# Two decode layers on one core: evacuation order, the place of the residual row, and what fills the waits between the layers

## The chip, the core and the metric

The kernel runs on one core of a Trainium2 chip, in one launch. The metric is the device time of that launch in microseconds. Everything is float32. Five engines work beside each other, each through its own instructions in program order: TensorE (PE) multiplies, VectorE (DVE) and ScalarE (ACT) do elementwise work, GpSimd (POOL) sets constants, and SyncE (SP) issues nearly all DMAs. They wait for each other by semaphores.

## The reference

Eight sequences (B = 8), one new token each, width D = 1024, go through the same pair of sublayers twice. Attention has 32 query heads over 4 key/value heads of size 128 and a cache of 4096 positions; the feed-forward width is 3584.

```
def _A_ref(x, k_cache, v_cache, wq, wo):
    q = (x @ wq) split into 32 heads of 128
    scores = q . k * Dh**-0.5;  p = softmax(scores);  o = p . v
    return o @ wo
def _B_ref(x, w1, b1, w2, b2):
    return gelu(x @ w1 + b1) @ w2 + b2
x = x + _A_ref(layernorm(x)); x = x + _B_ref(layernorm(x))
x = x + _A_ref(layernorm(x)); x = x + _B_ref(layernorm(x))
```

Both layers use the same weights and the same caches. The caches hold 8 x 4 x 4096 x 128 numbers each, 64 MiB per cache, and they are read in both layers, except for six value pieces of the last sequence that stay in SBUF.

## The kernel before, in words

**Memory.** One SBUF tile, the arena, is cut into 52 units of 1024 columns (4 KB in each of 128 partitions, 0.5 MiB in all). All weights and cache blocks come into it. A list, `stream`, names the transfers in the order in which they are issued, with the units where each may land; `pump` (L226) issues the head of the list once its units are free, and `release` (L238) frees the units of a block that has been read. All of it is decided while the program is built: on the chip, SP goes through a fixed order, and an issue waits for the last PE instruction that read the units. A transfer that waits therefore holds up all those behind it in the list.

**Rows.** Because there are only 8 sequences, a row vector of 1024 is held as `x_row`, 128 partitions by 256: the four column quarters lie under each other, 32 partitions each, of which 8 are used. Products are spread the same way: four matmuls that write to partitions 0, 32, 64 and 96 of one PSUM bank use the four column quarters of TensorE. The layer's input is also kept turned, in `xnT` (by `layernorm`, L192), 8 tiles of 128 x 8, which is what the matmuls take as their left side. PSUM is shared out as one bank each under the names "s" and "pt" and two under "o", and a bank is written again only after it has been read.

**Attention** (L578) goes sequence by sequence over k blocks (`scores`), a softmax (`probs`, `turn`) and v blocks (`values`, `heads`). `hooks` are functions put behind a named step. `project` (L334) multiplies with wo and adds to `x_row`.

**Feed-forward.** `expand` (L252) makes the 3584 hidden values in 7 groups of 512. For a group, eight matmul rounds over w1 write to `acc`; `flush` (L168) runs what is in `pending`; then DVE and ACT each copy one half of `acc` out of PSUM, scaled (L269, L270), into one of two row buffers, and the group's `hidden_group` (L319) is put in `pending`. `hidden_group` turns the row by four transposes on PE (L278) and does the bias and GELU in seven small steps on DVE and ACT (L324 to L330), which leaves `hT`. So a group's GELU is done behind the matmuls of the next group and ahead of its evacuation.

**The turn between the layers** is `swap` (L388). It works through four column blocks c of w2. Each block has 28 k tiles in three transfers: "u" (tiles 0 to 3), 0 (tiles 4 to 19) and 1 (tiles 20 to 27), in an order set by `W2_ORDER`. For a block, `down` (L367) does 28 matmuls (L371), DVE copies the result (L404), PE sums the partition groups (L406), and DVE adds it to the turned row (L408). One more matmul (L409) carries the block's result to the residual row, added to `x_row` at L430. The block gives two of the 8 k tiles of the next layer's query product, which is done at once by `q_part` (L287, L293) for two halves u: four pieces of wq in each block. wq has been in the arena since the start, and its units are what the next w2 blocks and then the next layer's k blocks are loaded into. The list behind the w1 groups is: w2 of blocks 0 to 3, k of the last sequence in several pieces, among them a rest of 64 KB of wq ("qe", unit 0, ahead of the third k piece), and so on. The k tile 7 of wq had to leave the arena: one half was parked in PSUM at the start (`park`, L616) and comes back by `unpark` (L623), an ACT copy and then a DVE copy, behind piece (3, 1), into the units that this piece frees; most of the other half is in `spare`, and the rest is "qe". `moments` (L450) forms the layer norm's statistics behind the last block, and the query rows are turned into `qz`.

**The bias b2.** `bias_row` (L351) builds the row b2 with products on PE and adds it to `x_row` in layer 0, behind the first group of `expand`; in layer 1 it writes to `b2_row`.

**Layer 1's feed-forward** has its w2 in the arena but for four "u" blocks of 0.5 MiB, which are the last transfers. `work` (L744) puts `grow(u - 1)`, the w2 products of a finished group, and `flush` behind a group's evacuation. Behind the last group come `grow_u(0, 1)`, the products of "u" for column quarters 0 and 1, then `flush` (the last group's turns and GELU), then `grow_u(2, 3)`; the last group's own products, the add (L748) and the store follow.

Of the kernel before, what the change touches and what calls it, by code (L numbers as in the profile page):

```python
# [8 lines left out]
F32 = mybir.dt.float32  # L9
# [5 lines left out]
P = 128  # L15
# [89 lines left out]
def decode_layers(ctx: ExitStack, tc: tile.TileContext, x, kc, vc, wq, wo, w1, w2, out):  # L105
# [12 lines left out]
    bits = const.tile([P, 2 + B + 2 * HQ + REP + T + 18], F32, name="bits")  # L118
# [8 lines left out]
    ones = ones.to_broadcast([P, P])  # L127
    epst = bit(1)
# [19 lines left out]
    xv = xv[:, :, 0:B]  # L148
    nc.gpsimd.memset(qz, 0.0)
# [42 lines left out]
    def layernorm(xr, rsum):  # L192
# [5 lines left out]
        shift = oxT[:, HQ * B + NT * XS + PAD:]  # L198
# [53 lines left out]
    def expand(name, rs, work={}):  # L252
        rows = [row_s, qz[:, 2 * GT * B:2 * GT * B + CH]]
        for u in range(NGR):
            acc = ps_o.tile([P, CH], F32, tag="o", name="acc")
            kt = 0
            for i, slot in enumerate(tiles((name, u))):
# [6 lines left out]
                flush()  # L264
# [3 lines left out]
            row = rows[u % 2]  # L268
            nc.vector.tensor_scalar(row[:, 0:CH // 2], acc[:, 0:CH // 2], rs, None, op0=ALU.mult)  # L269
            nc.scalar.activation(row[:, CH // 2:], acc[:, CH // 2:], AF.Copy, scale=rs)  # L270
            pending.append(lambda u=u, row=row: hidden_group(u, row))
# [79 lines left out]
    def bias_row(out, add, dg):  # L351
# [8 lines left out]
        if add is None:  # L360
            nc.vector.tensor_copy(out, y[:, 0:Q4])
        else:
            nc.vector.tensor_tensor(out, add, y[:, 0:Q4], ALU.add)
# [3 lines left out]
    def down(y, c, kts):  # L367

        for n, kt in enumerate(kts):
            g = kt % 4  # L370
            nc.tensor.matmul(y[32 * g:32 * g + 32], hT[:, kt * B:kt * B + 32], w2_at[c, kt], start=(n < 4), stop=(n >= NFT - 4))  # L371
# [16 lines left out]
    def swap():  # L388

        flush()  # L390
        ys = small_ps("s")
        nc.vector.tensor_tensor(xv, xv, b2T.unsqueeze(2).to_broadcast([P, NT, B]), ALU.add)
        pt = small_ps("pt")
        acc = q_acc()
        stats = ()
        for c in range(CB):
            y = ys[:, c % 2 * Q4:(c % 2 + 1) * Q4]
            kts = []
            for kind in W2_ORDER[c]:
                kts += arrive(c, kind)  # L400
            down(y, c, kts)
            release(held.pop(("w2u0", c)))
            ysb = row_s[:, c % 2 * Q4:(c % 2 + 1) * Q4]
            nc.vector.tensor_copy(ysb, y)  # L404
            for i in range(2):
# [3 lines left out]
            nc.tensor.matmul(pt[32 * c:32 * c + 32, Q4:2 * Q4], sel_x, ysb, start=True, stop=True)  # L409
            if c == CB - 1:  # L410
                stats = moments(pt)
            for kt in (2 * c, 2 * c + 1):
                for u in range(2):
                    if kt < NT - 1:
                        slot = held.pop(("q", kt, u))
                        q_part(acc, u, kt, 0, slot.ap)
                        release(slot)
                    elif u == 0:
                        q_part(acc, u, kt, 0, spot.ap)
# [399 lines left out]
```

## Time and profile before

| what | value |
|---|---|
| median of 3 runs | 862.34 us (861.06 to 862.88) |
| the profiled execution's own time | 861.24 us |
| its span in the profile | 859.5 us |
| mean granted TensorE clock | 0.803 |
| busy share PE, PEld, DVE, ACT | 63%, 22%, 23%, 7% |
| read from HBM | 358.83 MB, 418 GB/s over the span |

The profile is one execution. Times in it are microseconds from the start of the span. PE is matmuls, PEld is the loading of their left sides; an fp32 matmul shows as two records. In a row of the timeline stand the start, the time, the engine and line, the operation with output and inputs, the shapes and the number of instructions merged; brackets give the idle time before it and what ended it. In the chain of waits each row gives the start and length of what the end of the program hung on. In the table by windows, each engine has its busy time and its number of instructions, and the last three columns are PE's granted clock, the mean busy share of the 16 DMA engines and the rate.

### The profile page before, as it was taken

To read this page: it belongs to the slowest core of one execution; us is meant where nothing else is said; L and a number is where in the kernel's file an instruction comes from. 1 tells how busy PE (TensorE), PEld (TensorE's weight loads), DVE (VectorE), ACT (ScalarE), POOL (GpSimd) and SP (SyncE) were. 2 spreads that over 40 slices of the span, in tenths; PEclk is the share of its full clock that TensorE was granted. 3 is DMA by queue.
4 is the path that set the end of the run, shared out by engine and by line. 5 is a ranking of instruction groups with operands and counts; after the bars stand their busy time and mean duration, and the time that the engine had idled before them with its cause. 6 is when DMAs were issued, how large, how long until landed. Compare 5 with 4: busy or idle time off the path is not lost.

```text
span 859.5 us, 9291 instructions
## 1 busy us (share of the span) xinstructions
PE 540.7 (63%) x3986; PEld 186.6 (22%) x3986; DVE 199.9 (23%) x692; ACT 63.4 (7%) x136; POOL 2.1 (0%) x12
## 2 busy tenths in 40 slices
PE   0766655666655755756688676755656483664687
PEld 0221121121212121322233221111211121121233
DVE  0012231222212122301311332132222132231032
ACT  0110000000000000001101100000000000000020
POOL 0000000000000000000000000000000000000000
PEclk9976787867777777788889886679778687686899
DMA  9999999999999999999999999999999999999994
GB/s 397 432 422 436 432 422 435 425 432 423 432 436 423 432 434 427 425 426 427 416 362 420 378 434 424 445 423 435 428 429 422 432 426 438 430 444 419 422 421 167
DMA packets 19768, 359.55 MB, mean 418 GB/s; under 512 B 2192, under 2 KB 2576, under 8 KB 3600
## 3 DMA queue, kind: packets, MB, share of 16 engines
q1 hardware_dynamic: 19584, 358.82, 98.2%
q8 instruction: 31, 0.51, 0.2%
q10 hardware_dynamic: 144, 0.15, 0.0%
q14 instruction: 9, 0.07, 0.0%
HBM read 358.83 MB, written 0.13 MB: 418 GB/s over the span
## 4 chain that ended last, share of the span: by engine, by line
DMA 73%; PE 23%; DVE 1%; issue 1%; another core or an unknown queue 1%; ACT 0%; SPq 0%; ACTq 0%; DVEq 0%
DMA arena<-in_v_dram 27%; DMA arena<-in_k_dram 23%; DMA arena<-in_wo_dram 10%; PE o_ps L544 8%; DMA arena<-in_w_dram 7%; PE sps L488 7%; DMA arena<-in_wq_dram 6%; PE y L340 1%; PE sps L377 1%; PE acc L260 1%; PE acc L293 1%; PE sps L520 1%; PE sps L371 1%; PE sps L278 1%
## 5 line engine op out<-in xcount | busy, mean ns | idle before, releaser
L544 PE MATMUL o_ps<-arena 128*32 128x512 f32 x1024 | 169.4, 791 | 80.6 <-DMA arena<-in_v_dram 80.6
L488 PE MATMUL sps<-arena,qz 128*32 128x512 f32 x1024 | 149.6, 727 | 97.1 <-DMA arena<-in_k_dram 94.4
L488 PEld LDWEIGHTS sps<-arena,qz 128*32 128x32 f32 x1024 | 33.0, 126 | 180.0 <-DMA arena<-in_k_dram 101.4
L549 DVE SCALAR_TENSOR_TENSOR scr<-o_ps,bits,scr 128x128 f32<-128x128 f32 x192 | 67.4, 351 | 6.8
L544 PEld LDWEIGHTS o_ps<-arena 128*32 128x32 f32 x1024 | 34.2, 133 | 147.1 <-issue 113.9
L547 DVE TENSOR_SCALAR scr<-o_ps,bits 128x128 f32<-128x128 f32 x64 | 22.5, 351 | 173.0 <-PE o_ps L544 173.0
L511 ACT ACTIVATE arena<-arena,bits 128x512 f32<-128x512 f32 x32 | 22.8, 714 | 525.9 <-DVE scr L506 525.9
L340 PE MATMUL y<-arena,oxT 128*32 128x256 f32 x512 | 39.9, 469 | 32.8 <-DMA arena<-in_wo_dram 32.8
L493 DVE TENSOR_SCALAR_CACHE_REDUCE arena<-sps 128x512 f32<-128x512 f32 x32 | 22.1, 692 | 150.1 <-PE sps L488 150.1
L520 PE MATMUL sps<-ident,arena 128*128 128x128 f32 x128 | 29.6, 395 | 24.6 <-ACT arena L511 24.3
L260 PE MATMUL acc<-arena,oxT 128*32 128x512 f32 x224 | 34.0, 719 | 11.9 <-DMA arena<-in_w_dram 11.5
L293 PE MATMUL acc<-arena,oxT 128*32 128x512 f32 (+1 forms) x250 | 34.2, 657 | 7.1 <-DMA arena<-in_wq_dram 6.7
L556 PEld LDWEIGHTS sps<-bits,scr 128*128 128x128 f32 x128 | 21.1, 207 | 67.3 <-issue 38.4
L340 PEld LDWEIGHTS y<-arena,oxT 128*32 128x32 f32 x512 | 18.4, 130 | 51.9 <-DMA arena<-in_wo_dram 36.7
L520 PEld LDWEIGHTS sps<-ident,arena 128*128 128x128 f32 x128 | 21.3, 198 | 29.8 <-ACT arena L511 29.7
L557 DVE TENSOR_TENSOR oxT<-sps,scr 128x8 f32<-128x8 f32 x64 | 10.6, 165 | 72.1 <-PE sps L556 72.1
L556 PE MATMUL sps<-bits,scr 128*128 128x8 f32 x128 | 26.9, 283 | 0.0
L502 PE MATMUL sps<-scr,bits 128*128 128x128 f32 x32 | 8.3, 344 | 22.8 <-DVE scr L498 22.8
L524 DVE COPY arena<-sps 128x512 f32<-128x512 f32 x16 | 11.1, 692 | 30.4 <-PE sps L520 30.4
L377 PE MATMUL sps<-arena,oxT 128*32 128x256 f32 x224 | 16.9, 381 | 0.7 <-DVE oxT L330 0.6
L371 PE MATMUL sps<-arena,oxT 128*32 128x256 f32 x224 | 16.1, 412 | 1.4 <-DMA arena<-in_w_dram 1.4
L195 PE MATMUL sps<-ident,xb 128*128 128x128 f32 x6 | 1.5, 345 | 24.3 <-DMA xb<-in_x_dram 23.2
(116 smaller groups left out, 221.5 us busy)
## 6 DMA issues: line engine op xcount, KB each, us to landing
arena<-in_v_dram SPq DMA_DIRECT2D x19, 4096.0 KB, 19.3
arena<-in_k_dram SPq DMA_DIRECT2D x31, 2048.0 KB, 17.3
arena<-in_k_dram SPq DMA_DIRECT2D x12, 4096.0 KB, 17.5
arena<-in_w_dram SPq DMA_DIRECT2D x17, 2048.0 KB, 12.4
arena<-in_v_dram SPq DMA_DIRECT2D x4, 6144.0 KB, 25.0
arena<-in_v_dram SPq DMA_DIRECT2D x11, 2048.0 KB, 20.0
arena<-in_wo_dram SPq DMA_DIRECT2D x10, 2048.0 KB, 12.6
arena<-in_k_dram SPq DMA_DIRECT2D x2, 6144.0 KB, 23.4
```

What stands on the lines that cost most here:

```text
L260: nc.tensor.matmul(acc[32 * j:32 * j + 32, :], xnT[:, kt * XS:kt * XS + 32], slot.ap[:, c:c + G], start=(kt < 4), stop=(kt >= NT - 4))
L293: nc.tensor.matmul(acc[u][32 * j:32 * j + 32, d0 - j * CH:d1 - j * CH], xnT[:, kt * XS:kt * XS + 32], ap[:, d0 - c0:d1 - c0], start=(kt == ...
L340: nc.tensor.matmul(y[32 * j:32 * j + 32, 0:Q4], lhs[:, n * B:n * B + 32], slot.ap[:, c + j * Q4:c + (j + 1) * Q4], start=(n == 0), stop=(n ...
L371: nc.tensor.matmul(y[32 * g:32 * g + 32], hT[:, kt * B:kt * B + 32], w2_at[c, kt], start=(n < 4), stop=(n >= NFT - 4))
L377: nc.tensor.matmul(y[32 * c:32 * c + 32], hT[:, kt * B:kt * B + 32], w2_at[c, kt], start=st["y0"][c], stop=(kt == NFT - 1))
L488: nc.tensor.matmul(ps[32 * g:32 * g + 32, :], qz[:, c:c + 32], kt[:, g * CH:(g + 1) * CH], start=(j == 0), stop=(j == HKV - 1))
L511: nc.scalar.activation(part, part, AF.Exp, bias=bias, scale=1.0, accum_out=ls[:, h:h + 1])
L520: nc.tensor.transpose(pp[:, t * P:(t + 1) * P], row[:, c:c + P], ident)
L544: nc.tensor.matmul(o[32 * g:32 * g + 32, :], s[:, g], v[:, g * CH:(g + 1) * CH], start=(half == 0), stop=(half == NH - 1))
L547: nc.vector.tensor_scalar(r, o[:, 0:P], sel_t[:, 0:1], None, op0=ALU.mult)
L549: nc.vector.scalar_tensor_tensor(r, o[:, t * P:(t + 1) * P], sel_t[:, t:t + 1], r, op0=ALU.mult, op1=ALU.add)
L556: nc.tensor.matmul(po[:, 0:REP], r_s[j % 2], sel_h, start=True, stop=True)
```

## The change

Line numbers shift by a few; the prediction uses those of before.

1. `expand` takes `lag`. In layer 0 a group is evacuated first and `flush` (its predecessor's turns and GELU) follows. For group 0, the pending variance is flushed ahead of the evacuation, as before in both layers.
2. `swap` begins with the four "u" products of block 0, ahead of the `flush` that turns the last group.
3. Pieces (1, 1) and (3, 1) of wq are kept back (`late`) and done behind the next block's 28 products, between the issue of the DVE copy and the sums that read it. With (3, 1) goes its `unpark`, on ACT and DVE.
4. The product L409, the add L430 and layer 0's `bias_row` are gone. In layer 1 a new `rebuild` makes `x_row` from `xnT` by 16 matmuls of 32 x 128 and a DVE copy, behind the second value piece of the second sequence (number 6). It undoes the mean by a product with the row `shift`, kept now right behind the tiles of `xnT`, and a constant `share` of -1/128.
5. "qe" goes to unit 1 and is put in the list right behind w2, ahead of the k pieces.
6. In layer 1, the last group is turned directly behind its evacuation, and "u" is done for all four column quarters in one go behind it.

The order of the other transfers is as before.

```
-    def expand(name, rs, work={}):
+    def expand(name, rs, lag, work={}):
...
                 release(slot)
-                flush()
                 for f in work.get((u, i), ()):
                     f()
...
             row = rows[u % 2]
+            if u == 0:
+                flush()
             nc.vector.tensor_scalar(row[:, 0:CH // 2], acc[:, 0:CH // 2], rs, None, op0=ALU.mult)
             nc.scalar.activation(row[:, CH // 2:], acc[:, CH // 2:], AF.Copy, scale=rs)
+            if lag:
+                flush()
             pending.append(lambda u=u, row=row: hidden_group(u, row))
...
+    def rebuild():
+
+        ps = small_ps("s")
+        for kt in range(NT):
+            out = ps[32 * (kt // 2):32 * (kt // 2) + 32, kt % 2 * P:(kt % 2 + 1) * P]
+            nc.tensor.matmul(out, xnT[:, kt * XS:kt * XS + 32], ident, start=True, stop=False)
+            nc.tensor.matmul(out, xnT[:, NT * XS:NT * XS + 32], share, start=False, stop=True)
+        nc.vector.tensor_copy(x_row, ps[:, 0:Q4])
...
     def swap():
 
-        flush()
         ys = small_ps("s")
+        down(ys[:, 0:Q4], 0, arrive(0, "u"), 0)
+        flush()
...
+        def used(kt, u):
+            slot = held.pop(("q", kt, u))
+            q_part(acc, u, kt, 0, slot.ap)
+            release(slot)
+            if (kt, u) == (3, 1):
+                st["unparked"] = unpark()
...
             nc.vector.tensor_copy(ysb, y)
+            while late:
+                late.pop()()
             for i in range(2):
                 nc.tensor.matmul(pt[:, i * B:(i + 1) * B], ysb[:, i * P:(i + 1) * P], bsel, start=True, stop=True)
...
-            nc.tensor.matmul(pt[32 * c:32 * c + 32, Q4:2 * Q4], sel_x, ysb, start=True, stop=True)
...
                     if kt < NT - 1:
-                        slot = held.pop(("q", kt, u))
-                        q_part(acc, u, kt, 0, slot.ap)
-                        release(slot)
+                        late.append(lambda kt=kt, u=u: used(kt, u))
+                        if c == CB - 1 or (kt, u) not in ((1, 1), (3, 1)):
+                            late.pop()()
...
-                if kt == 3:
-                    spot = unpark()
-        nc.vector.tensor_tensor(x_row, x_row, pt[:, Q4:2 * Q4], ALU.add)
...
-    qe = (("qe", 0), 1, wq[0][:, -W:-KEEP], (0,), ())
+    qe = (("qe", 0), 1, wq[0][:, -W:-KEEP], (1,), ())
+    stream.append(qe)
     batch(1, last_b, ((4, 16), (4, 20), (4, 24), (2, 0), (2, 16)), ((4, 18),))
-    stream.insert([e[0] for e in stream].index((1, ("k", *k_at(last_b, 4)))), qe)
...
-            ("v", *v_at(last_b - 2, 0)): lambda: bias_row(b2_row, None, spare[:, Q4:Q4 + CH])}
+            ("v", *v_at(last_b - 2, 0)): lambda: bias_row(b2_row, spare[:, Q4:Q4 + CH]),
+            ("v", *v_at(last_b - 1, 1)): rebuild}
...
-            expand("i0", rs, {0: [lambda: bias_row(x_row, x_row, qz[:, 2 * GT * B:2 * GT * B + CH])]})
+            expand("i0", rs, True)
...
-                    (NGR - 1, 0): [lambda: grow(NGR - 2)], NGR - 1: [lambda: grow_u(0, 1), flush, lambda: grow_u(2, 3)]}
-            expand("i1", rs, work)
+                    (NGR - 1, 0): [lambda: grow(NGR - 2)], NGR - 1: [flush, lambda: grow_u(*range(CB))]}
+            expand("i1", rs, False, work)
```

More of the change, by code (lines that the diff above doesn't have):

```diff
@@ L117, in decode_layers @@
     make_identity(nc, ident)
-    bits = const.tile([P, 2 + B + 2 * HQ + REP + T + 18], F32, name="bits")
+    bits = const.tile([P, 3 + B + 2 * HQ + REP + T + 18], F32, name="bits")
     used = [0]
@@ L127, in decode_layers @@
     ones = ones.to_broadcast([P, P])
+    share = bit(1)
+    nc.gpsimd.memset(share, -1.0 / P)
+    share = share.to_broadcast([P, P])
     epst = bit(1)
@@ L359, in bias_row, with down @@
                 nc.tensor.matmul(y[32 * j:32 * j + 32, 0:Q4], ones[:, 0:32], dg[:, j % 2 * Q4:(j % 2 + 1) * Q4], start=True, stop=True)
[L360 to L363, printed above, removed]
+        nc.vector.tensor_copy(out, y[:, 0:Q4])
     w2_at = {}
-    def down(y, c, kts):
-        for n, kt in enumerate(kts):
+    def down(y, c, kts, n0=0):
+        for n, kt in enumerate(kts, n0):
             g = kt % 4
```

12 lines of the change are left out of this document (7 added, 5 removed).

## The prediction

> **What bounds the kernel now.** I read the page first: DMA in 40 slices, its queues, the shares of the chain that ended last.
>
> ```profile
> GB/s 397 432 422 436 432 422 435 425 432 423 432 436 423 432 434 427 425 426 427 416 362 420 378 434 424 445 423 435 428 429 422 432 426 438 430 444 419 422 421 167
> ...
> q1 hardware_dynamic: 19584, 358.82, 98.2%
> ...
> DMA 73%; PE 23%; DVE 1%; issue 1%; another core or an unknown queue 1%; ACT 0%; SPq 0%; ACTq 0%; DVEq 0%
> ```
>
> One queue moves 358.82 MB at a rate that hardly varies, so time is lost only where the rate falls: in slices 21 and 23 (362 and 378), and in the last slice (167), where the transfers end before the program does. Slices 21 and 23 are the turn between the layers (swap). The table by windows cuts it finer; its last columns are PE's granted clock, the DMA share and GB/s.
>
> ```profile
> core 0: us, PE busy (x) PEld busy (x) DVE busy (x) ACT busy (x) POOL busy (x), PEclk, DMA share, GB/s
> 430.62:434.03 3.41, 3.40 (x16) 0.59 (x16) 0.00 (x0) 0.09 (x1) 0.00 (x0) 0.50 1.04 436
> 434.03:437.45 3.42, 1.28 (x11) 0.71 (x8) 1.63 (x7) 0.70 (x2) 0.00 (x0) 1.00 0.96 407
> 437.45:440.86 3.41, 3.41 (x30) 1.54 (x34) 1.38 (x7) 0.23 (x1) 0.58 (x1) 0.50 1.04 442
> 444.50:450.00 5.50, 5.50 (x79) 2.40 (x72) 0.00 (x0) 0.00 (x0) 0.00 (x0) 1.00 0.70 222
> 476.00:478.00 2.00, 1.26 (x10) 0.30 (x2) 1.12 (x6) 0.60 (x2) 0.00 (x0) 1.00 0.92 291
> 482.00:490.00 8.00, 6.21 (x56) 2.07 (x56) 2.59 (x10) 0.00 (x0) 0.00 (x0) 1.00 0.98 334
> 510.00:660.00 150.00, 91.10 (x576) 28.18 (x568) 38.91 (x129) 8.46 (x20) 0.00 (x0) 0.77 1.01 431
> 660.00:810.00 150.00, 87.09 (x692) 30.72 (x688) 30.79 (x105) 6.35 (x15) 0.00 (x0) 0.77 1.00 429
> ```
>
> Against 429 GB/s the three dips lose 5.5 x (1 - 222/429) = 2.65 us, 2 x (1 - 291/429) = 0.64 us and 8 x (1 - 334/429) = 1.77 us: 5.07 us. From 510 to 810 the rate is 431 and 429: a transfer that starts earlier there stays earlier to the end.
>
> Why the first dip: the chain of waits in the turn, as it ended.
>
> ```profile
> 442.66 0.44 DVE scr L404
> ...
> 443.14 0.62 PE sps L406 x4
> ...
> 443.79 0.19 DVE oxT L408
> ...
> 444.02 0.40 PE sps L409
> 444.42 3.71 PE acc L293 x29
> ```
>
> After the first column block (its matmuls end at 442.66) PE waits 1.36 us for the copy, the sums and the add, spends 0.40 us on the residual's product (L409), and only then reads the four wq pieces (3.71 / 4 = 0.93 us each) whose slots the next w2 blocks need. The first of these is issued here, and the answer of the DMA view for that one issue gives its landing:
>
> ```profile
> 445.54 0.33 SPq L233 DMA_DIRECT2D arena<-in_w_dram  x1
> ```
> ```profile
> arena<-in_w_dram SPq DMA_DIRECT2D x1, 512.0 KB, 3.9
> ```
>
> 0.52 MB at 429 GB/s are 1.2 us; the other 2.7 us of the 3.9 are the most that lies between an issue and its data. So an issue must lead the end of the queued data by 2 to 2.7 us.
>
> **The change, part by part.**
>
> *Evacuation ahead of GELU (layer 0).* The turn's start:
>
> ```profile
> 434.15 0.66 PE L278 MATMUL sps<-ident,qz 128*128 128x128 f32 x4
> 436.24 0.48 DVE L269 TENSOR_SCALAR scr<-acc,bits 128x256 f32<-128x256 f32 x1
> 436.83 0.47 ACT L270 ACTIVATE scr<-acc,bits 128x256 f32<-128x256 f32 x1 [0.76 <-DVE scr L269]
> 437.93 4.65 PE L371 MATMUL sps<-arena,oxT 128*32 128x256 f32 x56
> ```
>
> The last group's matmuls end by 434.2; its rows leave PSUM at 436.24, behind the GELU of group 5. Now DVE goes at 434.2, ACT ends about 435.3, and the four turns end at 436.0 instead of 437.93. In between stand the four "u" products of block 0 (4 of 28). What is late next is a transfer:
>
> ```profile
> 427.69 0.33 SPq L233 DMA_DIRECT2D arena<-in_w_dram  x1
> ```
> ```profile
> arena<-in_w_dram SPq DMA_DIRECT2D x1, 2048.0 KB, 9.0
> ```
>
> These 16 w2 tiles land at 427.69 + 9.0 = 436.7, the next eight (1.05 MB, 2.44 us) at 439.2. The 28 products took 4.65 us, of which those up to 440.86 at clock 0.50: 2.93 / 2 + 1.72 = 3.19 us at full clock, 0.114 us each. Sixteen from 436.75 end at 438.6, eight from 439.2 at 440.1. That counts on full clock after 437.45: the rows above show 0.50 behind a window with 1.28 us of 3.42 busy and 1.00 behind one with 3.40; the window 434 to 437.45 will hold some 2.6 us. At half clock the end is 441.4. So block 0 ends 2.5 us (1.2) earlier; the hidden group 6 (1.5 us behind its turn, 437.6) is in time for its last four.
>
> The Trainium skill, "TensorE: Matmul & The Clock Gate", Part 1, has the half rate come only after at least one idle window of some 3.4 us. The trace differs: 1.28 us of work in 3.42 was not enough. By the rule, too, the clock would be full here, and block 0 would end at the same 440.1.
>
> *Residual rebuilt in layer 1.* L409 goes from all four blocks: 0.40 us each. The first wq-released issue comes 2.5 + 0.4 = 2.9 us sooner, 442.6; the dip had lost 2.65. In layer 1 sixteen products of 128 columns stand between two value pieces of batch 6. The trace has no such product; the nearest is this one, of 256 columns (two records to a product), with the idle time in front of a later PE group:
>
> ```profile
> L409 PE MATMUL sps<-scr,bits 128*32 128x256 f32 x8 | 2.9, 450 | 1.1 <-DVE oxT L408 1.1
> ```
> ```profile
> 551.26 8.13 PE L488 MATMUL sps<-arena,qz 128*32 128x512 f32 x48 [6.41 <-DMA arena<-in_k_dram]
> ```
>
> At 0.2 to 0.45 us each, 3 to 7 us of PE and one DVE copy of some 0.42. PE stands idle 6.41 us for k data soon behind it and DMA is full there, so I cost it at nothing; uncovered it is the 3 to 7 us. The bias row that layer 0 loses stood before group 1 of the expansion, which is paced by w1: nothing.
>
> *Waits filled with wq products.* Pieces (1,1) and (3,1) now stand on PE behind the next block's products, under the DVE copy. The queued data last until 445.0 to 446.2 (the rate falls in 444.5 to 450; 439.2 and 3.1 MB, 7.3 us, give 446.5 for the landing), block 1's last 0.5 MB until 446.2 to 447.4. The block at unit 6 is released by (1,1): about 449.1 (440.1 + 1.36 + three pieces = 444.3; block 1's products from there, the last when their tiles land at some 447.8; 0.4 and 0.93), and every later issue on SP queues behind it. Its cover is the 2.1 MB block ahead (4.9 us, until 451.1 to 452.3). With 2 to 2.7 us of lead that is 0 to 0.7 us short; with the start I leave 0.4 us of the first dip. Piece (3,1) also carries the unpark, in program order on DVE between block 2's copy and its add:
>
> ```profile
> 456.63 1.03 ACT L626 ACTIVATE arena<-spot 128x1024 f32<-128x1024 f32 x1 [17.36 <-PE acc L293]
> ```
> ```profile
> 457.69 1.23 DVE L627 COPY arena<-spot 128x1024 f32<-128x1024 f32 x1 [5.20 <-ACT arena L626]
> ```
>
> 0.93 + 1.03 + 1.23 = 3.2 us in place of 0.62 of sums: the add, and the wq pieces that release the first k blocks, come 2.6 us later in the block. Block 2's last tiles are drained 1.6 MB (3.7 us) later, 455.1 to 456.6, its products done 1.5 us behind, 456.6 to 458.1; 3.2 + 0.2 and two pieces (1.86) give the first k issue at 461.9 to 463.4. Block 3's three transfers (3.7 MB, 8.6 us) last until 463.7 to 465.2: a lead of 1.8, so 0.2 to 0.9 us short; I take 0.3.
>
> *The small wq piece (64 KB) ahead of the k blocks.* It now waits for block 2's products alone, which PE does before the pieces that the k blocks wait for, so it holds nothing up on SP. Before, it landed last of three:
>
> ```profile
> 465.99 13.02 DMA arena<-in_wq_dram
> ```
>
> Its product came at 479.06, so the query rows and the k slots that they free were late: the dip at 482 to 490. With everything some 6 us sooner, and the piece at hand, the next k issue (479.49 before) comes near 473, with data queued to about 479. That dip goes, 1.77 us; of the middle one I leave 0.2 us, since its rows are of 512 bytes still. **Turn: 5.07 - 0.4 - 0.3 - 0.2 = 4.2 us;** bounds 2.0 (each lead short by its worst, the block at half clock) and 5.1 (all three dips).
>
> *Last group turned at once.* The end of the chain, and DVE and ACT beside it:
>
> ```profile
> 845.88 1.93 PE sps L377 x32
> ...
> 848.67 2.60 PE sps L377 x16
> 851.27 0.59 PE sps L278 x4
> 851.86 4.48 PE sps L377 x48
> ...
> 856.36 0.42 DVE xb L748
> ```
> ```profile
> 848.74 0.48 DVE L269 TENSOR_SCALAR scr<-acc,bits 128x256 f32<-128x256 f32 x1 [2.92 <-PE acc L260]
> 849.32 0.47 ACT L270 ACTIVATE scr<-acc,bits 128x256 f32<-128x256 f32 x1 [3.75 <-DVE scr L269]
> ...
> 851.90 0.29 DVE L324 TENSOR_REDUCE qz<-sps 128x32 f32<-128x128 f32 x1 [2.67 <-PE sps L278]
> ...
> 853.19 0.19 DVE L330 SCALAR_TENSOR_TENSOR oxT<-qz 128x32 f32<-128x32 f32 x1
> ```
>
> Sixteen records on two of the four column quarters took 2.60 us, thirty-two on all four 1.93 us. Before: 2.60 + 0.59 + 4.48 from 848.67 to 856.34. After: PE idles until ACT's row at 849.79, turns until 850.3, does all four quarters of "u" in 1.93 (852.2), then group 6 in 1.93 (854.15), its GELU being done 1.5 us behind the turns, 851.8. **Tail: 2.2 us**; bounds 0.5 (half the gain of four quarters and a late w2 block) and 2.6.
>
> **Sum:** 4.2 + 2.2 = 6.4 us off the profiled execution's 861.24 us: 854.8. The median of the runs is 1.1 us above it: **855.9 us.**
>
> **The rivals.**
>
> *One dip stays (0.16).* DMA shares of 0.98 in 482 to 490 can be read as slow small transfers rather than an empty queue; 1.77 + 0.4 us stay: 858.1. The Trainium skill, "DMA: Bandwidth & Descriptors", Bandwidth, gives 341 GB/s at 1 MB; by that the dip of 334 would be size. Against it stands a stretch with w1 and w2 pieces of 1 and 0.5 MB:
>
> ```profile
> 842.00:844.00 2.00, 2.00 (x35) 1.13 (x28) 0.48 (x1) 0.47 (x1) 0.00 (x0) 1.00 1.01 406
> ```
>
> *The turn's gain is given back (0.06).* If a release on PE and not the queue paced layer 1, only the tail is left: 860.1; against it stand 431 and 429 GB/s.
>
> *No effect (0.03).* The 436.7 landing and the new waits eat the turn, the 1.1 us idle the tail: 862.
>
> *Slower (0.05): PE at half clock in the turn.* The unpark leaves PE idle for some 2 us in block 2. A window of 1.28 us busy was followed by 0.50; each 3.41 us window at half clock takes 1.7 us from a PE that every release waits for. Beyond the 2 us of lead and the 6.4 gained, it decides from five of the nine windows between 441 and 472; with seven, 11.9 - 8.4 = 3.5 us: 866. Against it: 1.00 in the turn's rows, and less idle time elsewhere.
>
> **How the numbers follow.** Forecast 0.70, rivals 0.16, 0.06, 0.03, 0.05. Bounds of the sum: 862.34 - 2.0 - 0.5 = 859.8 and 862.34 - 5.1 - 2.6 = 854.6, from which a median may lie 1.3 us off, as the lowest run of before does; 853.0 to 859.0 holds the forecast and the first rival. Measurement tells 0.2% (1.7 us) from no change; below 860.6 lie the forecast, the first rival and half of the second: faster 0.89, same 0.06, slower 0.05.
>
> **What would show it.** Right: 444 to 450 and 482 to 490 above 400 GB/s; block 0's copy near 440; one run of 32 records at the end in 1.93 us directly behind the last turns. Wrong: a new dip near 449 to 452 or 463 to 466 (c1, unpark), PEclk 0.50 between 441 and 472, or a rate under 425 behind 510.

## The result, and the profile after

The changed kernel takes 858.62 us (median of 6 runs, 856.96 to 860.23) beside 862.54 us of the kernel before (6 runs, 860.35 to 863.68): a ratio of 0.9956, interval 0.9938 to 0.9974. Measured a second time, on another chip and with 12 runs, it is 859.66 beside 860.93 us: 0.9980, interval 0.9966 to 0.9993. The intervals share 0.9966 to 0.9974, which is 2.2 to 2.9 us. So it is faster, as forecast. The first median lies inside the range of 853.0 to 859.0 and the second above it; of the 6.4 us of the sum 3.9 came by the first measurement, 1.3 by the second, and less than half by both together.

Line numbers are from here on those of the changed kernel: L299 was L293 (wq products), L383 was L371 and L389 was L377 (w2 products), L426 the copy, L430 the sums, L432 the add (L404, L406, L408 before), L647 and L648 the unpark (L626, L627), L236 the issues (L233). A run whose edit adds or drops lines has the later ones shifted by a few: where the add is at L430, the copy is L424.

The profiled execution took 858.83 us, its span is 856.9 us. The page first: rate in 40 slices, the queue, the shares of the chain that ended last.

```profile
GB/s 398 420 437 435 419 436 428 426 431 427 428 429 433 434 431 426 424 428 426 423 397 360 423 434 423 450 418 431 432 426 426 431 428 448 420 425 433 421 424 194
...
q1 hardware_dynamic: 19584, 358.82, 98.4%
...
DMA 72%; PE 23%; DVE 2%; issue 1%; ACT 1%; another core or an unknown queue 1%; SPq 0%; ACTq 0%; DVEq 0%
```

The bytes are the same. Slice 23 has gone from 378 to 423, but of the two low slices of the turn one is still there, and it has moved: slice 21 was 362 and slice 22 420; now they are 397 and 360. The table by windows shows where (last columns: PE's granted clock, DMA share, GB/s).

```profile
444.50:450.00 5.50, 4.58 (x71) 1.93 (x63) 0.42 (x1) 0.00 (x0) 0.00 (x0) 1.00 1.00 366
450.00:456.00 6.00, 4.95 (x60) 1.90 (x59) 0.17 (x1) 0.00 (x0) 0.00 (x0) 1.00 0.98 367
464.00:470.00 6.00, 6.00 (x56) 1.96 (x52) 0.00 (x0) 0.00 (x0) 0.00 (x0) 0.72 0.69 247
476.00:478.00 2.00, 1.91 (x20) 0.65 (x12) 1.15 (x5) 0.76 (x2) 0.00 (x0) 1.00 1.04 442
482.00:490.00 8.00, 5.36 (x52) 1.31 (x48) 1.14 (x4) 0.00 (x0) 0.00 (x0) 1.00 1.01 426
510.00:660.00 150.00, 92.19 (x620) 31.16 (x612) 40.88 (x136) 8.46 (x20) 0.00 (x0) 0.77 1.01 432
660.00:810.00 150.00, 86.40 (x688) 30.70 (x688) 29.70 (x102) 6.35 (x15) 0.00 (x0) 0.77 1.00 429
430.00:510.00 80.00, 64.33 (x586) 23.98 (x590) 21.86 (x79) 7.82 (x15) 0.58 (x1) 0.89 0.98 402
```

The rows of the kernel before for the windows that the prediction did not show:

```profile
450.00:456.00 6.00, 5.17 (x56) 2.17 (x50) 0.60 (x2) 0.00 (x0) 0.00 (x0) 1.00 0.97 407
464.00:470.00 6.00, 4.84 (x69) 1.88 (x61) 0.00 (x0) 0.00 (x0) 0.00 (x0) 1.00 1.02 431
430.00:510.00 80.00, 64.42 (x586) 25.74 (x590) 21.65 (x77) 8.18 (x15) 0.58 (x1) 0.89 0.98 397
```

All three dips of before are smaller or gone: 222 is now 366, 291 is 442, 334 is 426. A new one stands at 464 to 470, 431 before and 247 now: 6 x (1 - 247/429) = 2.55 us. The last row sums up the turn: 397 GB/s before, 402 now, that is 80 x (402 - 397) / 429 = 0.9 us of data. It is the measure by which the runs below are compared, since it counts the bytes of all sixteen DMA engines. (The landing of the first common value piece behind the turn, issued at 506.77 before and 506.12 after, is 526.90 and 524.25, 2.65 us apart; but the first of the sixteen engines is done with it at 523.25 and 522.38. In the profile of before the engines happen to lie further apart.)

The chain of waits through block 0, where the prediction wanted the copy near 440 and the first issue at 442.6:

```profile
440.46 0.44 DVE scr L426
...
441.59 0.19 DVE oxT L432
...
441.82 1.08 PE acc L299 x6
...
442.92 5.36 DMA arena<-in_w_dram
```

Copy at 440.46, no product for the residual row any more, first issue at 442.92 instead of 445.54: this step came as worked out. Block 2 did not. From its timeline:

```profile
459.30 1.94 PE L299 MATMUL acc<-arena,oxT 128*32 128x512 f32 x8
...
459.62 0.42 DVE L426 COPY scr<-sps 128x256 f32<-128x256 f32 x1 [9.04 <-PE sps L383]
...
461.16 0.61 PE L430 MATMUL sps<-bits,scr 128*128 128x8 f32 x4
461.26 1.02 ACT L647 ACTIVATE arena<-spot 128x1024 f32<-128x1024 f32 x1 [23.66 <-PE acc L299]
...
462.32 1.23 DVE L648 COPY arena<-spot 128x1024 f32<-128x1024 f32 x1 [2.28 <-ACT arena L647]
463.46 0.17 DVE L432 TENSOR_TENSOR oxT<-sps,oxT 128x16 f32<-128x16 f32 x1
...
463.68 3.67 PE L299 MATMUL acc<-arena,oxT 128*32 128x512 f32 x20 [1.91 <-DVE oxT L432]
...
466.54 0.33 SPq L236 DMA_DIRECT2D arena<-in_k_dram  x1
```

The sums behind the copy need 0.61 us, but the add that reads them comes 3.84 us behind the copy. Piece (3, 1) stands ahead of the sums on PE and runs at half speed, so they end at 461.77; and the add stands on DVE behind L648, which waits for ACT, which waits for piece (3, 1). That is the last 1.69 us. PE is idle for 1.91 us, and then reads the next wq pieces at half speed. The first transfer into k's places is issued at 466.54; the kernel before, with all else late, issued it at 463.84. A table cut to the windows of the clock shows the half speed:

```profile
454.50:457.75 3.25, 1.30 (x28) 0.56 (x24) 0.00 (x0) 0.00 (x0) 0.00 (x0) 1.00 0.99 378
457.75:461.16 3.41, 3.41 (x28) 0.61 (x19) 0.42 (x1) 0.00 (x0) 0.00 (x0) 0.50 1.07 453
461.16:464.57 3.41, 1.50 (x17) 0.81 (x17) 1.31 (x2) 2.31 (x2) 0.00 (x0) 1.00 0.97 406
464.57:467.99 3.42, 3.42 (x23) 0.85 (x19) 0.00 (x0) 0.00 (x0) 0.00 (x0) 0.50 0.62 184
```

Twice a window with 1.3 to 1.5 us of work is followed by one at clock 0.50; the second time it is the wait for the add that left PE idle.

The end of the chain:

```profile
845.09 0.90 PE acc L263 x8
...
846.01 0.49 DVE scr L273
...
846.59 0.48 ACT scr L274
...
847.12 0.44 PE sps L284 x2
847.56 6.26 PE sps L389 x64
...
853.85 0.42 DVE xb L770
```

From the last expansion matmul (845.99) to the end of the products (853.82) it is 7.83 us; before it was 7.67 (848.67 to 856.34). There is one run of records, as foretold, but not in twice 1.93 us: 6.26. The tail gained nothing.

The two spans differ by 2.6 us all the same. Most of the rest is in the sixteen DMA engines, which finish one transfer at different times. The end of the chain hangs on a w1 transfer; first the row of before, then that of after:

```profile
811.81 28.22 DMA arena<-in_w_dram
```
```profile
809.11 28.18 DMA arena<-in_w_dram
```

It has landed on the first engine at 835.10 before and 833.90 after, 1.2 us apart, and on the last at 840.03 and 837.29, 2.7 us apart. So some 1.5 us between these two profiles come from how far the engines lie apart at the end, and no step of the change is shown to make that.

The rebuild of the residual row, in layer 1:

```profile
528.52 0.64 PE L362 MATMUL sps<-ident,oxT 128*32 128x128 f32 x2
...
531.43 0.42 DVE L364 COPY xb<-sps 128x256 f32<-128x256 f32 x1 [1.57 <-PE sps L363]
```

It takes PE from 528.52 to some 531.4, and 510 to 810 runs at 432 and 429 GB/s as before (431, 429): hidden.

### The profile page after: what moved, and what is told of

The parts are those of the page before. It is cut to its first block, busy times and chain, and to the rows that moved or that the text cites. A ratio compares the mean times of both kernels' runs of the same rounds, so it can differ in the third digit from the quotient of the medians.

```text
span 856.9 us, 9313 instructions
## 1 busy us (share of the span) xinstructions
PE 539.4 (63%) x4002; PEld 185.5 (22%) x4002; DVE 198.8 (23%) x689; ACT 63.4 (7%) x136; POOL 2.2 (0%) x13
## 4 chain that ended last, share of the span: by engine, by line
DMA 72%; PE 23%; DVE 2%; issue 1%; ACT 1%; another core or an unknown queue 1%; SPq 0%; ACTq 0%; DVEq 0%
DMA arena<-in_k_dram 27%; DMA arena<-in_v_dram 22%; DMA arena<-in_wo_dram 10%; DMA arena<-in_w_dram 9%; PE sps L509 8%; PE o_ps L565 7%; DMA arena<-in_wq_dram 5%; PE acc L299 2%; PE y L346 2%; PE sps L389 1%; PE sps L541 1%; PE acc L263 1%; PE sps L383 1%; ACT arena L532 1%
## 5 line engine op out<-in xcount | busy, mean ns | idle before, releaser
L565 PE MATMUL o_ps<-arena 128*32 128x512 f32 x1024 | 165.8, 772 | 83.0 <-DMA arena<-in_v_dram 82.9
L299 PE MATMUL acc<-arena,oxT 128*32 128x512 f32 (+1 forms) x250 | 35.7, 707 | 6.6 <-DMA arena<-in_wq_dram 3.5
L383 PE MATMUL sps<-arena,oxT 128*32 128x256 f32 x224 | 14.8, 398 | 4.4 <-DMA arena<-in_w_dram 4.4
L389 PE MATMUL sps<-arena,oxT 128*32 128x256 f32 x224 | 15.9, 380 | 0.6 <-DVE oxT L336 0.6
```

The source lines that it names most:

```text
L299: nc.tensor.matmul(acc[u][32 * j:32 * j + 32, d0 - j * CH:d1 - j * CH], xnT[:, kt * XS:kt * XS + 32], ap[:, d0 - c0:d1 - c0], start=(kt == ...
L389: nc.tensor.matmul(y[32 * c:32 * c + 32], hT[:, kt * B:kt * B + 32], w2_at[c, kt], start=st["y0"][c], stop=(kt == NFT - 1))
L565: nc.tensor.matmul(o[32 * g:32 * g + 32, :], s[:, g], v[:, g * CH:(g + 1) * CH], start=(half == 0), stop=(half == NH - 1))
```

## The experiments

Each is an edit of the changed kernel. "Beside" is the median of the kernel before on the same chip. The table gives, from each profile, block 2's copy, its add, the first transfer into k's places (us of the span), PE's clock in 456 to 464 and 464 to 470, the rate from 430 to 510, and the last run of 64 records.

| run | copy | add | first k issue | clock | GB/s 430 to 510 | 64 records | median, beside | ratio, interval |
|---|---|---|---|---|---|---|---|---|
| before | 460.10 | 461.23 | 463.84 | 1.00, 1.00 | 397 | - | 862.54 | - |
| changed | 459.62 | 463.46 | 466.54 | 0.79, 0.72 | 402 | 6.26 | 858.62, 862.54 | 0.9956 (0.9938 to 0.9974) |
| changed_again | 459.35 | 462.35 | 464.55 | 1.00, 1.00 | 411 | 6.26 | 859.66, 860.93 | 0.9980 (0.9966 to 0.9993) |
| tail_old | 459.44 | 462.43 | 465.42 | 0.98, 0.75 | 409 | - | 858.32, 861.15 | 0.9971 (0.9958 to 0.9983) |
| tail_wide | 459.98 | 463.83 | 467.75 | 0.70, 0.54 | 396 | 3.63 | 857.53, 861.15 | 0.9953 (0.9936 to 0.9971) |
| wide_only_31 | 460.52 | 463.51 | 466.88 | 1.00, 0.72 | 401 | 3.63 | 856.94, 860.41 | 0.9957 (0.9942 to 0.9972) |
| unpark_later | 458.42 | 459.76 | 461.98 | 1.00, 0.99 | 414 | 6.26 | 857.56, 861.15 | 0.9955 (0.9942 to 0.9968) |
| no_late | 459.45 | 460.58 | 462.80 | 1.00, 1.00 | 416 | 6.26 | 856.72, 861.15 | 0.9949 (0.9936 to 0.9961) |
| both_mended | 460.79 | 462.13 | 464.35 | 0.79, 1.00 | 412 | 3.63 | 854.97, 860.88 | 0.9927 (0.9912 to 0.9942) |
| wide_no_late | 457.91 | 459.04 | 461.25 | 1.00, 1.00 | 422 | 3.64 | 854.11, 860.93 | 0.9929 (0.9915 to 0.9944) |
| wide_later_no_late | 457.81 | 458.94 | 461.16 | 1.00, 1.00 | 423 | 3.82 (x63) | 854.95, 860.93 | 0.9936 (0.9921 to 0.9951) |

**The changed kernel once more** (no edit).

> The changed kernel once more, to have it beside the two below. The unpark stands ahead of block 2's add: both theories expect the first transfer into k's places at 465 to 467.8 us of the span (466.54 in its first profile), a dip below 345 GB/s in 464 to 470, and the first transfers common to both kernels behind the turn 1.2 to 4 us earlier than before. Ratio 0.9940 to 0.9970. If the dip of its first profile was chance, the first such transfer would come at 462 to 463.5 and the dip would be gone.

The first k issue came at 464.55, between the two expectations, and the ratio, 0.9980, above the one expected. The clock was full in the whole turn, but the add was 3.0 us behind its copy again, and the dip is there, if less deep than expected: 366 GB/s from 464 to 470. So the dip is not a chance of the first profile, and with the add held it was deepest where the clock was lowest (224 in tail_wide). The two ratios of this one kernel, 0.9956 and 0.9980, also say how much a single ratio is worth here.

**The end of layer 1 as before** (tail_old).

```
-  NGR - 1: [flush, lambda: grow_u(*range(CB))]}
+  NGR - 1: [lambda: grow_u(0, 1), flush, lambda: grow_u(2, 3)]}
```

> The changed kernel with the end of layer 1 as before: u for quarters 0 and 1, the last group's turns, u for quarters 2 and 3. The prediction's theory (turning at once gains 2.2 us): 860.8. The reading of the two traces (from the last expansion matmul to the end of the products 7.67 us before and 7.82 us after; the 1.1 us that PE idles for the evacuation eat what the earlier GELU gives): 858.4 to 858.6, no difference.

The chain of its last 8 us:

```profile
845.06 2.60 PE sps L389 x16
...
848.25 4.48 PE sps L389 x48
```

With 0.59 us of turns between them these are the terms of before, 7.67 us, beside 7.83 of the changed kernel. Undoing part 6 of the change costs nothing that is measured: 0.9971 lies between the two ratios of the changed kernel.

**All four quarters of "u" together** (tail_wide). `grow_u` walks through the quarters c and does each one's products before the next; the edit waits for all four and gives them to `down_row` at once.

```
                 for c in cs:
                     arrive(c, "u")
-                    down_row(y[0], groups[0], [c])
+                down_row(y[0], groups[0], cs)
```

> The changed kernel, but the last products of the u blocks run over the k tiles outside and the column quarters inside, instead of one quarter after the other. Theory (one quarter at a time keeps three quarters of the array idle): the 32 records of u, 3.57 us in the changed kernel's trace, take about 1.9; with some 0.6 us of waiting for the last u block the run of 64 records ends 1.6 to 1.8 us sooner, the whole at about 857.0 where the changed kernel has 858.6. Rival (the order of quarters does not matter, the records are bound by something else such as the loading of the left sides): the run of 64 records stays at 6.3 us and the time at 858.6.

```profile
849.06 3.63 PE sps L389 x64
```

The same 64 records take 3.63 us instead of 6.26, now that neighbours write to different column quarters; nothing else was changed. That is 2.4 to 2.6 us off the end in every run that has the edit. The ratio does not show it here: this profile's turn was the worst of those with the turn of the changed kernel (396 GB/s, clock 0.70 and 0.54).

**The unpark behind block 2's add** (unpark_later), (1, 1) and (3, 1) still kept back.

```
-            if (kt, u) == (3, 1):
-                st["unparked"] = unpark()
...
             nc.vector.tensor_tensor(xc, pt[...], xc, ALU.add)
+            if c == 2:
+                st["unparked"] = unpark()
```

> The changed kernel, but the copies that bring back the parked wq half are issued behind block 2's add instead of ahead of it. Theory A (these copies hold up the add, and with it the pieces that release the first k block): the add comes about 1.6 us sooner behind the block's copy, PE's idle time of 1.9 us in front of the next pieces goes, the first k issue moves from 466.5 to between 463.3 and 464.9, and the dip at 465 to 469 (2.6 us lost) shrinks to under 1: time 856.3 to 857.3. Theory B (the late arrival of block 2's second transfer, issued at 449.9 behind the kept-back piece, makes the dip): the first k issue stays past 465.5 and the time at 858.2 to 858.6.

Its timeline in block 2:

```profile
458.42 0.43 DVE L424 COPY scr<-sps 128x256 f32<-128x256 f32 x1 [8.20 <-PE sps L383]
...
459.76 0.18 DVE L430 TENSOR_TENSOR oxT<-sps,oxT 128x16 f32<-128x16 f32 x1 [0.92 <-PE sps L428]
...
461.98 2.04 SPq L236 DMA_DIRECT2D arena<-in_k_dram  x2
```

and one row of its table by windows:

```profile
464.00:470.00 6.00, 3.88 (x60) 2.06 (x60) 0.82 (x3) 0.00 (x0) 0.00 (x0) 0.99 1.05 430
```

The add is 1.34 us behind its copy, the first k issue 3.56 us behind it instead of 6.92, and the dip at 464 to 470 is gone. Beside changed_again, whose clock was full there too, it is 3.56 against 5.20 us and 430 against 366 GB/s. Nothing else was changed, so the unpark's place made the delay. The time does not show it by itself: 857.56 us is above the 856.3 to 857.3 expected, and 0.9955 is the changed kernel's first ratio. The turn as a whole is at 414, for 470 to 482 runs at 385 and 380, with a half-clock window at 469.9 to 473.3.

**No piece kept back** (no_late).

```
-                        if c == CB - 1 or (kt, u) not in ((1, 1), (3, 1)):
-                            late.pop()()
+                        late.pop()()
```

> The changed kernel without the keeping back: pieces (1,1) and (3,1) are done at once again, as in the kernel before, with the unpark behind (3,1) in block 1. Theory A and B together (what was put into the waits releases units too late and brings the unpark into the way): block 2's second transfer is issued near 445.6 instead of 449.9, the first k issue comes near 461 to 462 instead of 466.5, and neither the dip at 452 to 456 nor that at 465 to 469 is there: 855.0 to 856.0. Rival (the filling pays): two pieces of 0.93 us less under the copies, about 0.5 us later in each of blocks 1 and 2, the dips as they are: 859 to 860.

This puts two things back: (1, 1) is read in its own block, so block 2's piece is issued at 446.20 instead of 449.88; and the unpark runs while PE waits for block 2's tiles (L647's copy on DVE at 455.42, the block's copy at 459.45), so it holds up no add. The first k issue comes 3.35 us behind the copy, and the turn is at 416 GB/s. One dip that was expected to go is still there: 464 to 470 is at 343. The copy was late for another reason. Block 2's last w2 transfer landed on half of the sixteen DMA engines by 456.46, but on the last at 458.68; in wide_no_late below, with the same turn, these are 456.28 and 457.13, the copy 457.91 and the window 432. So a held add is not the only thing that makes the k issue late. Which of the two edits counts is asked next.

**Only (3, 1) kept back** (wide_only_31, with the four quarters together).

```
-                        if c == CB - 1 or (kt, u) not in ((1, 1), (3, 1)):
+                        if c == CB - 1 or (kt, u) not in ((3, 1),):
...
-                    down_row(y[0], groups[0], [c])
+                down_row(y[0], groups[0], cs)
```

> All four quarters of u in one run of records; piece (1,1) is done in its own block, and only (3,1), with its unpark ahead of block 2's add, is still kept back. This stands between the run with both kept back and the one with none, and parts two costs. Theory that the kept-back release (1,1) is the larger: block 2's piece is issued at 445 to 446.5 instead of 449.9, its copy comes at 457 to 458, the add still 3.8 us behind it, the first transfer into k's places at 463.5 to 464.5, some 2 to 2.7 us ahead of the end of the queued data: 464 to 470 above 400 GB/s, 430 to 510 at 414 to 421, ratio 0.9925 to 0.9945. Rival, that the add held behind the unpark is the larger: 464 to 470 below 370 GB/s, 430 to 510 at 402 to 412, ratio 0.9945 to 0.9970.

The theory put on record as the first fell. The piece was issued early, 446.58, yet the copy came at 460.52 and the rest as in the changed kernel:

```profile
460.52 0.42 DVE L426 COPY scr<-sps 128x256 f32<-128x256 f32 x1 [9.60 <-PE sps L383]
...
462.37 1.22 DVE L648 COPY arena<-spot 128x1024 f32<-128x1024 f32 x1 [1.43 <-ACT arena L647]
463.51 0.17 DVE L432 TENSOR_TENSOR oxT<-sps,oxT 128x16 f32<-128x16 f32 x1
...
466.88 0.33 SPq L236 DMA_DIRECT2D arena<-in_k_dram  x1
```

From the copy to the first k issue it is 6.36 us, 464 to 470 is at 289 GB/s, and the 430 to 510 rate of 401 is that of the runs with both pieces kept back. The late copy itself has another cause: block 0 ran at half clock (437.0 to 440.4), its first issue came at 443.98 instead of 442.92, and block 2's last transfer landed at 459.74. The delay behind the copy is the one that unpark_later removes: 5.20 to 7.77 us in the five profiles with the add held, 3.34 to 3.56 in the five without. So the add held behind the unpark, with the half clock that came with it, is the larger cost in the turn, and the release of (1, 1) at most the smaller.

**Unpark behind the add and four quarters together** (both_mended: the edits of unpark_later and tail_wide).

> The changed kernel with two mends: the unpark copies behind block 2's add, and the u products over all four column quarters at once. If the two causes are the ones (2.2 us of the turn, where the unpark delays the first k issue, and 2.6 us at the end, where the run of 64 records went from 6.26 to 3.63), they add: the turn gains 4.2 to 4.8 us on the kernel before and the end 2.5 to 2.8, ratio 0.991 to 0.9925 (some 854 against 861.2). If the one hides the other (the end waits for the last u transfer, which the earlier turn cannot move alone), 0.994 to 0.995.

0.9927, 5.9 us below the kernel before on the same chip and just above the range expected; the turn gained 80 x (412 - 397) / 429 = 2.8 us, not 4.2 to 4.8, in a profile with a half-clock window at 456.8 to 460.2. With the four quarters in both, the add held gives 0.9953 and 0.9957 (tail_wide, wide_only_31), the add free 0.9927, 0.9929 and 0.9936 (this run and the next two): some 2 us.

**Nothing kept back and four quarters together** (wide_no_late: the edits of no_late and tail_wide).

> All four quarters of u in one run of records, and no release kept back, with the unpark still ahead of block 2's add. Theory that the kept-back release (1,1) starves block 2: the piece of block 2 is issued at 446.2 instead of 449.9, the first transfer into k's places comes at 462.5 to 463.5 and the turn gains 4 to 4.8 us, the end 2.4 to 2.7: ratio 0.9915 to 0.9935. Rival, that the unpark's place ahead of the add is what makes it late: 465 or later, turn 1.2 to 2.7, ratio 0.9945 to 0.9960.

Two rows of its table by windows and one of its chain:

```profile
430.00:510.00 80.00, 63.28 (x602) 23.88 (x606) 22.72 (x81) 7.82 (x15) 0.58 (x1) 0.93 1.01 422
464.00:470.00 6.00, 4.56 (x64) 2.13 (x60) 0.87 (x3) 0.00 (x0) 0.00 (x0) 1.00 1.03 432
```
```profile
844.72 3.64 PE sps L389 x64
```

854.11 us, 6.8 below the kernel before. The first k issue is at 461.25, a little before what the prediction had worked out for the changed kernel (461.9 to 463.4).

**All three edits** (wide_later_no_late).

> All three edits: four quarters of u together, the unpark behind block 2's add, and no release kept back. If the unpark and the kept-back release cost one and the same wait of block 2, the two mends do not add: first transfer into k's places 460.5 to 462.5, ratio 0.9910 to 0.9930, that of the unpark's mend with the four quarters (0.9927) within 0.0015. If they are two costs, 1.5 us more: ratio 0.9895 to 0.9912.

0.9936, within 0.0015 of 0.9927: the mends do not add. First k issue 461.16 and 423 GB/s beside 461.25 and 422; both remove one and the same wait.

The last three runs undo one further part of the change each, on top of both_mended, and are compared with it (854.97 us, same chip).

**The small wq piece ahead of the third k block again** (small_piece_last).

```
-    qe = (("qe", 0), 1, wq[0][:, -W:-KEEP], (1,), ())
-    stream.append(qe)
+    qe = (("qe", 0), 1, wq[0][:, -W:-KEEP], (0,), ())
...
+    stream.insert([e[0] for e in stream].index((1, ("k", *k_at(last_b, 4)))), qe)
```

> The two mends, with the 64 KB wq piece back in its old place ahead of the third k block. The prediction's theory (its late landing makes the dip at 482 to 490, 1.77 us): its product comes 2 us or more later, the dip is back, 1.5 to 2 us slower than with both mends. Rival (the dip came from the whole turn being late; with the first k blocks in time there is a cover of 2 to 3 us): piece some 2 us later, no dip over 0.6 us, 0 to 0.6 us slower.

```profile
479.91 0.42 PE L299 MATMUL acc<-arena,oxT 128*32 128x128 f32 x1 [3.75 <-DMA arena<-in_wq_dram]
```
```profile
482.00:490.00 8.00, 6.89 (x60) 3.19 (x63) 3.62 (x14) 0.57 (x1) 0.00 (x0) 0.93 0.84 330
```

858.06 us, 0.9963 (0.9951 to 0.9976): 3.1 us more than both_mended, where 1.5 to 2 were expected. PE waits 3.75 us for the piece, and the dip of before is back, 330 GB/s in 482 to 490 where both_mended has 436. That dip is 8 x (436 - 330) / 429 = 2.0 us; this profile's turn was slower ahead of it too, with half clock at 459.2 to 466.0, which the piece is not shown to make.

**Evacuation behind GELU, "u" of block 0 behind the last turns** (evacuation_behind).

```
                 release(slot)
+                flush()
...
-            if lag:
-                flush()
...
-        ys = small_ps("s")
-        down(ys[:, 0:Q4], 0, arrive(0, "u"), 0)
         flush()
+        ys = small_ps("s")
```

> The two mends, with layer 0's evacuation behind the predecessor's GELU and block 0's u products behind the last turns, as before. Theory (this step moves block 0 by 2.2 to 2.5 us and with it the first wq-released issue): block 0's copy at 442.6 or, with the clock full, 441.4; the first such issue at 444 to 445.1 instead of 442.9; the dip at 444 to 450 is back with 1.5 to 2.3 us; 1.5 to 2.3 us slower than with both mends. Rival (the next transfers pace the turn anyhow): under 0.7 us slower.

```profile
443.06 0.44 DVE scr L420
...
445.52 4.50 DMA arena<-in_w_dram
```

856.50 us, 0.9942 (0.9925 to 0.9959): 1.5 us more, the intervals overlap. The copy is at 443.06 and the first issue at 445.52, where both_mended has 441.17 and 443.62, and 444 to 450 is at 229 GB/s (381 in both_mended): the first dip is back.

**The residual row in the turn** (residual_in_turn): L409's product and the add of before, `bias_row` in layer 0, no `rebuild`.

```
+            nc.tensor.matmul(pt[32 * c:32 * c + 32, Q4:2 * Q4], sel_x, ysb, start=True, stop=True)
...
+        nc.vector.tensor_tensor(x_row, x_row, pt[:, Q4:2 * Q4], ALU.add)
...
-            ("v", *v_at(last_b - 1, 1)): rebuild}
```

> The two mends, with the residual row kept up in the turn as before (a product of 256 columns in each block, the add, and the bias row in layer 0; no rebuilding in layer 1). Theory: 0.40 us more in each block ahead of its wq pieces, first wq-released issue 0.4 us and first k issue up to 1.2 us later; 0.4 to 1.0 us slower than with both mends. Rival (the rebuilding in layer 1, 2.5 us of PE, costs something too): the same time as with both mends or faster.

```profile
442.25 0.40 PE sps L436
```

856.29 us, 0.9942 (0.9926 to 0.9958): 1.3 us more, the intervals overlap. The chain shows its 0.40 us in block 0 in the way of the wq pieces.

## Why the prediction was right in sign and too large in size

**The number.** Both terms of the sum came out below their own lower bounds: the turn at 0.9 to 1.4 us where 2.0 was the least, the tail at -0.16 where it was 0.5. That the first median is inside the range is therefore luck, as is its nearness to the 858.1 of the first rival: the dip that this rival keeps, 482 to 490, is gone. The two terms give some 1.2 us, which is the second measurement's 1.3; why the first has 3.9 stays open. Of the prediction's own signs, 482 to 490 is above 400 GB/s and block 0's copy came near 440; but 444 to 450 is at 371, the run at the end is not 1.93 us, and a dip behind 463 and windows at clock 0.50, which were to show it wrong, are there.

**The turn: 4.2 us forecast.** By the prediction's own account, on its windows: of the first dip 5.5 x (1 - 366/429) = 0.81 us stay, and 450 to 456 loses 6 x (1 - 367/429) = 0.87 instead of 0.31, so 1.4 us where it left 0.4; the dips at 476 and 482 to 490 leave 0.06 where it left 0.2; and block 2 loses 2.55 us where it took 0.3. That is 5.07 - 1.4 - 0.06 - 2.55 = 1.1 us, in agreement with 0.9 from the rate over the whole turn. The four profiles with the changed turn have 402, 411, 409 and 396 GB/s, mean 404.5: 80 x (404.5 - 397) / 429 = 1.4 us (-0.2 to 2.6). The five with the rest of the change and no add that waits for the unpark have 412 to 423, mean 417.4: 3.8 us. So the failed step is the one on piece (3, 1) and the unpark, "I take 0.3".

Its working held in kind. It had the add behind the unpark and the later release, and named 463 to 466 as the place of a new dip. It went wrong in three places of one sum. The copy was put at 456.6 to 458.1 and came at 459.62. From the copy to the start of the wq pieces it had 3.2 + 0.2 us; the rows give 463.68 - 459.62 = 4.06, because the (3, 1) piece runs at half clock before the unpark. Two pieces were to take 1.86 us and took 466.54 - 463.68 = 2.86, at half clock again. Together: 3.1 us behind the late end of its bracket, at a place where it had found a lead of 1.8 us, already 0.2 us short. The kernel before had none of this: unpark at 457.69, copy at 460.10, first k issue 3.74 us behind it; the changed kernel needs 6.92, 5.20, 5.98 and 7.77 in its four profiles.

**The clock.** The rival that ended slower was this mechanism, and it needed five half-clock windows or more between 441 and 472 to decide. None (changed_again) to four (tail_wide) occurred, and from copy to issue it is 5.20 us with none and 7.77 us in tail_wide. The right use would have been a term of the sum, by estimate: an idle stretch of 2 us ahead of PE work that a release waits for may be paid with up to 1.7 us more, half a window of 3.41. In the turn of these profiles each stretch of half clock begins behind a window in which PE had at most 2.1 us of work, but such a window does not always bring it: in wide_only_31 one with 1.49 us (454.09 to 457.50) was followed by full clock. That the clock explains the whole spread between 396 and 411 GB/s is only argued.

**The lead of (1, 1).** The release came at 449.88 (449.1 forecast) and 450 to 456 fell to 367. The runs without it are no better when the unpark stays ahead of the add (401). With the unpark behind the add, keeping the pieces back (both_mended) or not (wide_later_no_late) gives 412 and 423 GB/s but 0.9927 and 0.9936, so no cost in time is shown. What this one edit costs by itself stays open: it is less than the spread between profiles.

**The tail: 2.2 us forecast, -0.16 measured.** The failed step is "does all four quarters of 'u' in 1.93". The hidden groups' products walk over the quarters inside each k tile, but `grow_u` does one quarter after the other, as the code of before already showed (its 16 records in 2.60 us were two quarters one after the other, not two at once). The idle time of PE for DVE and ACT, 1.1 us, was in the sum. With the four together the tail is 5.21 us (843.15 to 848.36 in wide_no_late), 2.46 less than before: the size was about right for the kernel that had been read into the diff.

**What was right.** The evacuation (copy at 440.46, first issue 442.92; undone, the first dip returns); the small wq piece (undone, the dip at 482 to 490 and its 2.0 us return, with transfers of the same sizes in both, so that dip came from the piece's late landing and not from the sizes); the residual row (0.40 us in a block, the rebuild hidden); the layer behind (432 and 429 GB/s, so what the turn gains stays). With part 3 left out and the four quarters together the kernel is at 854.11 us and 0.9929; the forecast of 855.9 beside 862.34 had been 0.9925, which speaks for the steps left and not for part 3.

## What to carry to other kernels

When a step is moved into a wait, list what stands behind its last instruction on every engine that it touches: here the matmuls filled PE's wait, but two copies went with them, and the second stood on DVE, behind the first on ACT, ahead of the very add that everything waited for. Read the loop order of the helper that a reordered call uses before giving its products a price: the same 64 matmul records took 6.26 or 3.63 us by which loop was outside. And on an engine that every release waits for, price an idle stretch of 2 us as itself and a slow window behind it.

## What was not expected of the hardware

- Half clock comes in windows of 3.41 us that begin at other places in each profile: 457.75 and 464.57 in the changed kernel, 456.8 in both_mended, none between 440 and 470 in changed_again, with the same instructions as the changed kernel. The Trainium skill, "TensorE: Matmul & The Clock Gate", Part 1, has the window free-running, not reset by a kernel's start; the traces agree as far as they show it, since the windows of the two profiles of the changed kernel stand at different places of one and the same program, which had 402 and 411 GB/s over the turn. Windows with as little as 1.30 and 1.50 us of work were followed by 0.50, but one with 1.49 (wide_only_31) by 1.00.
- A run of matmul records with outputs of 32 partitions depends on its order: 32 records of "u" cost 6.26 - 1.93 = 4.3 us one quarter after the other and 3.63 - 1.93 = 1.7 us with the quarters in turn, where 1.93 us is the row of 32 records of a hidden group.
- The sixteen DMA engines finish one transfer at different times: for the first value piece behind the turn the first and the last are 3.65 us apart in the profile of before and 1.87 in that after; for the w1 transfer at the end it is 4.93 and 3.39. A landing read from one profile is uncertain by that much.
